# First out phase in 128x128 products with bursts of scores; nine loads of later quads moved behind the second out phase

## The chip, the cores and the metric

The kernel runs on one core of a Trainium2 chip. The metric is the device time of one execution in microseconds, the median of several runs. A core has five engines with queues of their own: PE (TensorE, matmuls), DVE (VectorE), ACT (ScalarE), POOL (GpSimd) and SP (SyncE). Here POOL issues the loads from HBM and SP the stores and the transposing DMAs.

## The reference

Sigmoid attention over 8 batches, 12 heads, 448 positions and 64 columns a head, followed by a feed-forward layer with a SiLU:

```
scores = q @ k.T / sqrt(64) - log(448)          per batch and head
x      = sigmoid(scores) @ v                    heads side by side: 3584 x 768
h      = x @ w_in                               768 x 2048
out    = (h * sigmoid(h)) @ w_out               2048 x 768, float32
```

The kernel holds its operands in float16 and sums in float32.

## The kernel before

**Attention.** The heads of a batch are taken four at a time, a quad: 24 quads, three to a batch. A quad's k and q come in by DMA (`kf`, `qf`, four buffers each), are copied into another order (`kr`, `qr`, L166, by DVE or ACT) and transposed by a DMA on SP's queue (`kT`, `qT`, L167). Scores come in tiles, seven to a quad (`scores`, L173): four matmuls of 64x64 with 448 columns fill one of two score buffers `psc` (L182), and ACT's sigmoid (L189) turns it into `attnT`, of which there are twelve. When a quad has its seven tiles, 28 matmuls of 64x64 (a set of value matmuls, L214) multiply them by v (`vf`, three buffers) into two banks `pav`, and DVE or ACT move these to `xT` (L226, L230).

**Feed-forward.** It goes by pairs of batches, m = 0 to 3. An h stage makes `gTr`, the SiLU of h; an out phase multiplies it by `w_out`. For m = 0 the h stage is plain (`h_unit`, L285, 128x128 matmuls `ph` of 448 columns, 189 ns a step); from m = 1 it is `h_pair` (L345), which forms the four blocks of a product by seven products of sums (`hx`, `hy`, `hz`, L361), as the out phase does as well: a set of seven products of 8 steps each (`out_set`, L491), with sums `S1` to `S4` of blocks of `gTr` made by DVE before them (`jobs`, L501) and the results gathered in `osb` by DVE (`plus`, L514; `end1` to `end7`). There are three sets in an out phase, and a fourth for m = 1 and 3. The fifth product of a set writes to `osb[1]`.

**Two forms of a product.** `alone` (L601) runs one product as 8 matmuls of 128x128 with 384 columns. `two` (L624) runs two products side by side as 64 matmuls of 64x64 (`side_by_side`, L248, L264), 16 steps of four. An attention tile, also 64x64, can be put between any two steps of a pair. In the kernel before only the first `FIRST_ALONE[m]` = 1 products of an out phase, and what is left over at its end, run alone (the last phase, without attention, wholly).

**The order** is written out by the program: `all_moe` is a generator that emits the feed-forward step by step with an estimate of its ns (163 a product step, 189 an h step), and the code around it emits attention tiles between the steps. Batches 0 and 1 come first, and attention of batches 2m and 2m + 1 is then laid into the h stage and the out phase of the pair before. Two ways of laying it in matter here:

- bursts (`bursts_to`, `attend`, `share`, L925 to L950): two tiles at once, or two tiles, the value set of a full quad and a third tile, then a stretch of dense steps, the stretches sized so that the bursts are evenly spread. They are used among 128x128 work.
- `deal` (L864): one tile at a time between the steps of pairs, by a due time and an estimate of when ACT is free (`sigmoid[-2]`), with a value set at the turn of a pair.

Before, the attention of batches 2 and 3 (46 tiles: quads 6 to 11 and four tiles of quad 12) starts with six tiles in bursts within the h stage and goes on by `deal` through the first out phase. The other phases use `deal`.

**Loads.** When q of quad g has been transposed, POOL makes a copy of one element (`seen`, L799), which waits for that transpose, and then issues k and q of quad g + 3. When the value set of quad g is emitted, `after_values` (L775) issues v of quad g + 3. In `h_pair` the first four rounds each emit one k or q copy of the coming quads (`late`, L376), k by ACT.

DVE's sums for the next set are emitted in `ended` (L587), as soon as the product that frees their buffer ends.

Of the kernel before, what the change touches and what calls it, by code (L numbers as in the profile page):

```python
# [19 lines left out]
def kernel(  # L20
# [140 lines left out]

    def dma_transpose(g, name, copy):
        if ("k", g) not in qkT:
            new_qkT(g)
        rows = p2.tile([P, NCH, 2, D], F16, tag=f"{name}r", name=f"{name}r")
        copy(rows, flat[name, g].rearrange("p j c d -> p c j d"))  # L166
        nc.sync.dma_start_transpose(  # L167
            out=qkT[name, g], in_=rows.rearrange("p c j d -> p (c j d)")
        )
# [294 lines left out]
    def w_sums():  # L464
# [3 lines left out]
        for f0 in range(0, NHC, NHC // 2):  # L468
            for o, x, y in (
# [5 lines left out]
                for f in range(f0, f0 + NHC // 2, 2):  # L475
                    nc.vector.tensor_sub(o[:, f : f + 2], x[:, f : f + 2], y[:, f : f + 2])
                    yield

    kept = cpool.tile([P, NFC, P], F16, tag="kept", name="kept")

# [10 lines left out]
    def out_set(a1, rows1, a2, rows2, scale, tail=(), last=False, halves=False, early5=False):  # L491
# [90 lines left out]
        return products, jobs  # L582

    free = {1: 0, 2: 0, 3: 0, 4: 0}
    jobs_to_do = []

    def ended(products):  # L587
        nonlocal vector_at
        for product in products:
            if product[5]:  # L590
                free[product[5]] += 1
        while jobs_to_do and free[jobs_to_do[0][0]] > 0:
            tag, job = jobs_to_do.pop(0)
            free[tag] -= 1
            job()
            vector_at = max(vector_at, clock) + 700
        while chores:
# [26 lines left out]
    def two(products, extras):  # L624
# [20 lines left out]
        yield 163  # L645

    rows_at = {14: (6, "k"), 16: (6, "q"), 18: (7, "k"), 21: (7, "q")}
    early = [h_unit(0, fc) for fc in range(2)]
# [27 lines left out]
    def out_products(m, tail):  # L676
        scale = ISX if m == 0 else 1.0
        for g in (0, 2, 4):
            of_set, jobs = out_set(
# [10 lines left out]
            for i, product in enumerate(of_set):  # L690
                extra = None
                if m % 2 == 0 and g == 2 and i < 4:
                    extra = partial(keep_part, scale, i)
                elif m == 0 and g == 2:
                    extra = partial(next, in_sums)
                elif m == 0 and g == 0 and i < 3:
                    extra = partial(list, islice(sums, 2 if i == 0 else 1))
                yield product, extra
        if m % 2 == 1:
# [9 lines left out]
            jobs_to_do.extend(jobs)  # L709
            for product in of_set:  # L710
                yield product, None

    def all_moe():
        for m in range(B // 2):
            tail = []
# [18 lines left out]
    def stretch(ns):  # L734
        nonlocal done, due
        due += ns
        while done < due or hold:
            step_ns = next(stream, None)
            if step_ns is None:
                break  # L740
            done += step_ns

    first_q = load_first_q()
# [31 lines left out]
    def after_values(g):  # L775
# [8 lines left out]
        elif g == 2:  # L784
# [11 lines left out]
    def rows_of_quad(g, name, copy):  # L796
        dma_transpose(g, name, copy)
        if name == "q" and g + 3 < NQB:
            nc.gpsimd.tensor_copy(seen, qkT["q", g][:1, NCH - 1, P - 1 :])  # L799
# [6 lines left out]
    def rows_if_any():  # L806
        if later:
            rows_of_quad(*later.pop(0), nc.vector.tensor_copy)

# [54 lines left out]
    def deal(n, stop, end, lead):  # L864
# [18 lines left out]

        for at in range(n, stop):
            due = start + (end - start) * (at - n + AHEAD) / (stop - n)
            while True:
                turn()
                if place == "turn" and room():
                    break
                if room() and done >= due and (clock >= sigmoid[-2] or done >= due + SLIP) and not hold:  # L890
                    break
                if place == "end":
                    rows_if_any()
                    place = None
                advance()
            between = place == "turn"
            if at % 2:
                rows_if_any()
# [9 lines left out]
            if ch == NCH - 3 and g % 6 < 4 and g + 3 < NQB:  # L908
                later.extend(((g + 3, "k"), (g + 3, "q")))
            if between and waiting and clock >= max(waiting[0][1], banks_at):  # L910
# [6 lines left out]
    def advance():  # L917
        nonlocal done, clock
        ns = next(stream)
        done += ns  # L920
        clock += ns

    AHEAD, SIGMOID, SLIP, DEBUG = 0.5, 850, 1e9, 0
    SWITCH, TILE, ROUND, SPARE = 200, 190, 190, 2400
# [39 lines left out]

    FIRST_ALONE = {0:1,1:1,2:1,3:1}
    WAIT = {1: 0, 2: 1300, 3: 1300}
    EXTRA = {1: 4, 2: 4, 3: 0}
    IN_H, LEAD, BEFORE = 6, {1:0,2:2600,3:2600}, {1:3200,2:2600,3:3000}
    sets = 7 * NHC * 163
    h_at = (2 * NFC * NCC - 8) * 189 + 3 * sets  # L970
    n = 2 * NT_B
    for m in range(1, B // 2):
        stop = min(2 * (m + 1) * NT_B + EXTRA[m], len(units))
        if m == 1:
            bursts = bursts_to(n, n + IN_H)
            for at, (burst, full) in enumerate(bursts):
                attend(burst, full)
                if at:
                    rows_if_any()
                if at == 1:  # L980
                    rows_if_any()
                for g, ch in burst:
                    n += 1
# [12 lines left out]
        seen_pairs = pairs_of  # L996
        while m < B // 2 - 1 and pairs_of == seen_pairs:
            advance()
# [33 lines left out]
```

## Time and profile before

| | us |
|---|---|
| runs | 361.05, 360.62, 360.23; median 360.62 |
| profiled execution | 362.33 |
| its span, first to last instruction | 360.6 |
| granted TensorE clock | 1.00 throughout |
| first h stage, with bursts (from 23.3) and dense | 23.3 to 74.5 |
| first out phase (m = 0) | 74.5 to 123.0 |
| second h stage (`h_pair`) | 123.0 to 156.2 |
| second out phase (m = 1) | 156.2 to 212.0 |
| third h stage | 212.0 to 245 |
| third out phase (m = 2) | 245 to 288 |
| fourth h stage and last out phase, no attention left | 288 to 360.6 |

The stages are read from the starts of PE's matmuls. Busy time of PE is the modelled time of its matmuls, which overlap, so rates are better read from start to start; "PEld" are weight loads. "issue" as a releaser means that the engine waited for nothing the profile shows. The DMA share is the mean busy share of the 16 DMA engines and can exceed 1, since packets overlap. Queue 0 carries POOL's loads, queue 1 SP's stores and transposes, queue 8 PE's instructions.

### The profile page before, as it was taken

What the parts mean: (1) busy time and instruction counts of PE and PEld (TensorE: products, weight loads), DVE (VectorE), ACT (ScalarE), POOL (GpSimd) and SP (SyncE); (2) the same over time, 40 slices, a digit from 0 to 9 for tenths busy, and PEclk for the clock granted to TensorE, in tenths of its full rate; (3) what the DMA queues carried; (4) which work ended last, traced back from release to release, by engine and by line L of the source; (5) the groups of instructions that cost most, each with busy time, mean ns of one, the idle gap of its engine ahead of it and who ended that gap; (6) DMA issues with size and microseconds to landing.
All of it is one profiled execution on the core that took longest, in us unless ns stands there. A gap on an engine that the chain in (4) does not pass through costs nothing.

```text
span 360.6 us, 10787 instructions
## 1 busy us (share of the span) xinstructions
PE 348.8 (97%) x4605; PEld 214.2 (59%) x4605; DVE 259.9 (72%) x487; ACT 247.5 (69%) x363; POOL 62.4 (17%) x105
## 2 busy tenths in 40 slices
PE   8999999999989999999997999999999999999995
PEld 4544445467777555567775765556787745555653
DVE  2547689897695578787755758787866677787663
ACT  5998977778776677687885667759889766660000
POOL 8545300604223001102203200210110000000000
PEclk9999999999999999999999999999999999999999
DMA  8999999999999446306899952731795030003333
GB/s 136 198 206 205 210 207 196 167 182 128 207 159 234 86 97 105 53 2 114 159 133 212 193 116 51 104 51 31 83 188 115 4 87 2 0 0 90 87 89 87
DMA packets 63919, 43.00 MB, mean 119 GB/s; under 512 B 36096, under 2 KB 60928, under 8 KB 63872
## 3 DMA queue, kind: packets, MB, share of 16 engines
q0 software_dynamic: 24896, 22.58, 42.3%
q1 hardware_dynamic: 38592, 19.21, 28.8%
q8 instruction: 36, 0.59, 0.7%
q10 hardware_dynamic: 384, 0.52, 0.4%
q14 instruction: 11, 0.09, 0.1%
HBM read 45.61 MB, written 11.01 MB: 157 GB/s over the span
## 4 chain that ended last, share of the span: by engine, by line
PE 88%; ACT 7%; issue 2%; DMA 1%; DVE 1%; ACTq 0%; POOLq 0%
PE po L264 21%; PE po L609 12%; PE hy L361 11%; PE ph L285 11%; PE psc L182 9%; PE pav L214 8%; PE hx L361 8%; PE hz L361 8%; ACT attnT L189 6%; DMA kf<-in_k_dram 1%; PE ptrq L151 1%; DVE osb L514 1%; PE ptrk L151 1%; DVE qT L158 0%; ACT m L529 0%
## 5 line engine op out<-in xcount | busy, mean ns | idle before, releaser
L189 ACT ACTIVATE attnT<-psc 128x896 f16<-128x896 f32 x168 | 143.5, 928 | 27.3 <-PE psc L182 26.1
L264 PEld LDWEIGHTS <-S 64*64 64x64 f16 x1248 | 58.2, 107 | 13.6 <-issue 2.8
L182 PE MATMUL psc<-qT,kT 64*64 64x448 f16 x672 | 64.1, 355 | 1.3 <-DVE qT L158 0.4
L264 PE MATMUL po<-T,S 64*64 64x384 f16 x640 | 53.2, 323 | 0.2 <-issue 0.2
L264 PEld LDWEIGHTS <-gTr 64*64 64x64 f16 x800 | 43.1, 107 | 9.6 <-issue 2.3
L514 DVE SCALAR_TENSOR_TENSOR osb<-po,osb 128x384 f32<-128x384 f32 x70 | 37.6, 554 | 15.0 <-PE po L264 9.7
L264 PE MATMUL po<-w_out_sb,S 64*64 64x384 f16 x608 | 44.6, 323 | 1.3 <-issue 1.2
L361 PEld LDWEIGHTS <-w_in_sb 128*128 128x128 f16 x288 | 28.0, 98 | 26.5 <-issue 0.6
L372 ACT ACTIVATE gTr<-u 128x448 f16<-128x448 f32 x48 | 27.6, 575 | 23.1 <-DVE u L385 19.1
L230 DVE TENSOR_SCALAR xT<-pav 128x448 f16<-128x448 f32 x44 | 25.6, 619 | 23.5 <-PE pav L214 23.5
L264 PE MATMUL po<-w_out_sb,gTr 64*64 64x384 f16 x480 | 40.5, 324 | 1.0 <-issue 1.0
L214 PE MATMUL pav<-attnT,vf 64*64 64x448 f16 x672 | 39.4, 350 | 2.0 <-issue 1.9
L285 PE MATMUL ph<-xT,w_in_sb 128*128 128x448 f16 x192 | 39.0, 353 | 0.0
L182 PEld LDWEIGHTS <-kT 64*64 64x64 f16 x672 | 26.5, 105 | 17.9 <-issue 10.9
L361 PE MATMUL hy<-xs,w_in_sb 128*128 128x448 f16 x144 | 35.1, 352 | 0.0
L264 PE MATMUL po<-T,gTr 64*64 64x384 f16 x320 | 34.3, 323 | 0.7 <-issue 0.7
L361 PE MATMUL hx<-xT,w_in_sb 128*128 128x448 f16 x144 | 34.6, 353 | 0.0
L361 PEld LDWEIGHTS <-W 128*128 128x128 f16 x216 | 21.1, 98 | 19.9 <-DVE osb L514 0.5
L214 PEld LDWEIGHTS <-vf 64*64 64x64 f16 x672 | 23.4, 106 | 10.9 <-issue 4.5
L514 DVE SCALAR_TENSOR_TENSOR osb<-po,m 128x384 f32<-128x384 f32 x32 | 17.2, 554 | 16.8 <-ACT m L529 6.4
L285 PEld LDWEIGHTS <-w_in_sb 128*128 128x128 f16 x192 | 17.6, 98 | 18.8 <-issue 3.6
L91 POOL DMA_DIRECT2D vf<-in_v_dram x24 | 17.1, 716 | 52.2 <-PE psc L182 42.6
(84 smaller groups left out, 481.0 us busy)
## 6 DMA issues: line engine op xcount, KB each, us to landing
out_dram<-osb SPq DMA_DIRECT2D x46, 192.0 KB, 4.0
vf<-in_v_dram POOLq DMA_DIRECT2D x24, 224.0 KB, 7.4
kf<-in_k_dram POOLq DMA_DIRECT2D x23, 224.0 KB, 6.1
qf<-in_q_dram POOLq DMA_DIRECT2D x23, 224.0 KB, 7.0
w_in_sb<-in_moe_w_in_dram POOLq DMA_DIRECT2D x8, 384.0 KB, 11.4
w_out_sb<-in_moe_w_out_dram POOLq DMA_DIRECT2D x4, 768.0 KB, 17.0
out_dram<-osb SPq DMA_DIRECT2D x17, 96.0 KB, 2.2
kT<-kr SPq DMA_TRANSPOSE x18, 5.8
```

Source lines behind the costliest of these rows:

```text
L91: nc.gpsimd.dma_start(flat[name, g][:, :, c0:c1].rearrange("p j c d -> p j (c d)"), rows_in(name, g)[:, :, c0 * D : c1 * D],)
L151: nc.tensor.matmul(ptr[j * D : (j + 1) * D, (c - c0) * P : (c - c0 + 1) * P], flat[name, g][:, j, c, :], ident, start=True, stop=True,)
L182: nc.tensor.matmul(psc[own, j, :S], qkT["k", g][rows, ch, own], qkT["q", g][rows, :, own], start=True, stop=True,)
L189: nc.scalar.activation(attnT[g, ch], psc[:, :, :S], AF.Sigmoid, bias=NEG_LOG_S, scale=QKSCALE)
L214: nc.tensor.matmul(pav[half][j * D : (j + 1) * D, :S], flat["v", g][own, j, ch, :], at[own, j, :], start=(ch == 0), stop=(ch == NCH - 1),)
L230: nc.vector.tensor_scalar_mul(xT[b][:, half * NQ + iq, :], pav[half][:, :S], SX)
L264: mm = nc.tensor.matmul(ps[lane ^ turn][own], a[rows, own], b[rows], start=(turn == c == 0), stop=(turn == 1 and c == count - 1), skip_gro ...
L285: nc.tensor.matmul(ph[:, :S], w_in_of[:, cc // NQ, cc % NQ, fc * P : (fc + 1) * P], xT[b][:, cc, :], start=(at == 0), stop=(at == NCC - 1),)
L361: nc.tensor.matmul(ps, a[:, c, i * P : (i + 1) * P], bs(c), start=(first and c == 0), stop=(c == HCC - 1), skip_group_check=True,)
L372: nc.scalar.activation(gTr[:, side * NHC + i, odd * S : (odd + 1) * S], src, AF.Silu, scale=ISX)
L514: nc.vector.scalar_tensor_tensor(out=o, in0=po, scalar=sign * scale, in1=x, op0=ALU.mult, op1=ALU.add)
L609: nc.tensor.matmul(po, a[:, fc, :], w[:, fc, :], start=(fc == 0), stop=(fc == NHC - 1))
```

## The change

In the first out phase all 21 products run alone, in 128x128 matmuls, and all 46 tiles of batches 2 and 3 are laid in as bursts (20 of them: four in the h stage, sixteen in the out phase). The loads of k and q of quads 19, 20, 21 and of v of quads 18, 19, 20 no longer follow the transposes and value sets of the second out phase: POOL issues them one after the other during the last product of its last set, behind a copy of one element of `osb[1]` (`mark`), which waits for that set's fifth product. v of quads 16 and 17 are issued after the value sets of quads 14 and 15 instead of 13 and 14. DVE's sums are emitted at the fourth step of a product, at most two at a time, and in the first and last out phase also when a product ends; extras move from the third to the fourth step. `deal` asks for at least one step between two tiles, and in the second out phase starts 400 ns earlier. Names that have no effect as set (`HALVES`, `GRID`, `EASE`, the parts of a transpose) are left out below.

```diff
+            first_done.append(osb[1])                     # in end5
...
+    AT_STEP, PER_TURN, prompt = 3, 2, False
     def ended(products):
         for product in products:
             if product[5]:
                 free[product[5]] += 1
-        while jobs_to_do and free[jobs_to_do[0][0]] > 0:
+        if prompt:
+            sums_if_any(4)
+
+    def sums_if_any(most):
+        while most and jobs_to_do and free[jobs_to_do[0][0]] > 0:
             tag, job = jobs_to_do.pop(0)
...
-            if fc == 2 and extra:
-                extra()
+            if fc == AT_STEP:
+                if not between:
+                    sums_if_any(2)
+                if extra:
+                    extra()
...
-            if at in (2, NHC + 2) and extras[at // NHC]:
-                extras[at // NHC]()
+            if at in (AT_STEP, NHC + AT_STEP):
+                sums_if_any(PER_TURN)
+                if extras[at // NHC]:
+                    extras[at // NHC]()
...
+                yield product, partial(load_behind, m) if m in BEHIND and i == BEHIND_AT else None
...
+            prompt = m in PROMPT
...
-        elif 4 < g < NQB - 3:
+        elif 4 < g < NQB - 3 and g not in VALUES_OF:
             load("v", g + 3)
+        for of in VALUES_OF.get(g, ()):
+            load("v", of)
...
+    BEHIND = {1: (("kq", 19), ("kq", 20), ("kq", 21), ("v", 18), ("v", 19), ("v", 20))}
+    VALUES_OF = {13: (), 14: (16,), 15: (17,), 16: (), 17: ()}
+    def load_behind(m):
+        nc.gpsimd.tensor_copy(mark, first_done[-1][:1, :1])
+        for names, g in BEHIND[m]:
+            load(names, g)
...
-        if name == "q" and g + 3 < NQB:
+        if name == "q" and g + 3 < NQB and g + 3 not in BEHIND_KQ:
             nc.gpsimd.tensor_copy(seen, qkT["q", g][:1, NCH - 1, P - 1 :])
...
-                if room() and done >= due and (clock >= sigmoid[-2] or done >= due + SLIP) and not hold:
+                if room() and done >= due and moved and (clock >= sigmoid[-2]) and not hold:
...
-    FIRST_ALONE = {0:1,1:1,2:1,3:1}
-    WAIT = {1: 0, 2: 1300, 3: 1300}
+    FIRST_ALONE = {0: 21, 1: 1, 2: 1, 3: 1}
+    PROMPT, WAIT, BURSTS = (0,3), {1: 0, 2: 900, 3: 1300}, (1,)
...
-        if m == 1:
-            bursts = bursts_to(n, n + IN_H)
+        if m in BURSTS:
+            bursts = bursts_to(n, stop)
             for at, (burst, full) in enumerate(bursts):
                 attend(burst, full)
...
-                    stretch(share(bursts[at:], 2 * NFC * NCC * 189 - 8 * 189 - 1134 - 400 - done))
-            while 1 not in h_done or place != "turn" and done < 0:
-                advance()
-        deal(n, stop, h_at - BEFORE[m], LEAD[m])
+                    stretch(share(bursts[at:], h_at - SPARE - done))
+        else:
+            deal(n, stop, h_at - BEFORE[m], LEAD[m])
```

More of the change, by code (lines that the diff above doesn't have):

```diff
@@ L596, in ended @@
             vector_at = max(vector_at, clock) + 700
+            most -= 1
         while chores:
@@ L734, in stretch @@
     def stretch(ns):
-        nonlocal done, due
+        nonlocal done, due, clock
         due += ns
@@ L807, in rows_if_any @@
         if later:
-            rows_of_quad(*later.pop(0), nc.vector.tensor_copy)
+            g, name, *part = later.pop(0)
+            rows_of_quad(g, name, nc.vector.tensor_copy, *part)
     keep_busy(0, 4)
@@ L889, in deal @@
                     break
-                if room() and done >= due and (clock >= sigmoid[-2] or done >= due + SLIP) and not hold:
+                if room() and done >= due and moved and not GRID < since < 16 and (clock + EASE >= sigmoid[-2]) and not hold:
                     break
@@ L908, in deal @@
             if ch == NCH - 3 and g % 6 < 4 and g + 3 < NQB:
-                later.extend(((g + 3, "k"), (g + 3, "q")))
+                later.extend(
+                (g + 3, name, *part)
+                for name in "kq"
+                for part in (((0, 4), (4, NCH)) if m in HALVES else ((),))
+            )
             if between and waiting and clock >= max(waiting[0][1], banks_at):
@@ L917, in advance @@
     def advance():
[L918 removed]
+        nonlocal done, clock, since
         ns = next(stream)
         done += ns
+        since = 0 if place == "turn" else since + 1
         clock += ns
[L923 removed]
+    AHEAD, SIGMOID, GRID, EASE, DEBUG = 0.5, 850, 99, 0, 0
+    since = 0
     SWITCH, TILE, ROUND, SPARE = 200, 190, 190, 2400
@@ L996 @@
         seen_pairs = pairs_of
-        while m < B // 2 - 1 and pairs_of == seen_pairs:
+        if m + 1 in BURSTS:
+            due = done
+            stretch(3000)
+        while m < B // 2 - 1 and m + 1 not in BURSTS and pairs_of == seen_pairs:
             advance()
```

43 lines of the change are left out of this document (29 added, 14 removed).

## The prediction

> **What bounds it now.** I read the page first: who is busy, what the last chain is made of, and the DMA queues.
>
> ```profile
> PE 348.8 (97%) x4605; PEld 214.2 (59%) x4605; DVE 259.9 (72%) x487; ACT 247.5 (69%) x363; POOL 62.4 (17%) x105
> ...
> q8 instruction: 36, 0.59, 0.7%
> ...
> PE 88%; ACT 7%; issue 2%; DMA 1%; DVE 1%; ACTq 0%; POOLq 0%
> ```
>
> TensorE (PE) carries the kernel, so the time is its work plus the stretches in which it starts nothing. The small "issue" share is time in which PE waits for nothing the profile names. Next the windows, one per out phase that has attention work in it:
>
> ```profile
> core 0: us, PE busy (x) PEld busy (x) DVE busy (x) ACT busy (x) POOL busy (x), PEclk, DMA share, GB/s
> 74.50:123.00 48.50, 45.54 (x978) 34.32 (x977) 36.22 (x74) 37.43 (x47) 12.15 (x21) 1.00 1.15 168
> 156.20:212.20 56.00, 53.54 (x1178) 39.37 (x1178) 38.82 (x76) 41.28 (x52) 10.58 (x18) 1.00 0.83 135
> 245.00:288.00 43.00, 42.66 (x962) 32.59 (x960) 30.97 (x63) 36.89 (x48) 2.11 (x3) 1.00 0.57 88
> ```
>
> PE idles about 3 us in the first and 2.5 us in the second, 0.3 us in the third; the DMA share (1.15, 0.83, 0.57) falls in the same order. The chain, asked for stretches of the first and second, says where:
>
> ```profile
> 103.65 0.46 PE po L264 x9
> 104.11 0.98 issue
> 105.08 0.51 PE po L264 x6
> ...
> 111.17 0.76 issue
> ...
> 117.81 0.68 issue
> ```
>
> ```profile
> 189.05 1.12 issue
> 190.17 1.30 PE pav L214 x21
> ...
> 196.06 1.22 issue
> ```
>
> These stops have one cause, read from two lists. Counted along PE's own list of instructions (9,241, weight loads included), the six longest stops of the out phases fall at positions 2498, 2755, 3010, 3267 and 5315, 5570: always 256 (within 2) or a multiple apart. Queue 8 moves 36 packets of 16,384 bytes, and 36 x 256 = 9,216, so one packet is 256 instructions. The packets of these stops landed at 96.88, 103.56, 110.36, 117.20, 188.88 and 195.76 us, and PE went on 1.3 to 1.6 us after each. So PE had run out of instructions. A packet started about when PE passed the place 256 earlier where there was little other traffic (within 0.7 us of it at 161.34, 178.23 and 246.51), but 4.0 to 4.6 us after it in these six cases, where loads, stores and transposes filled the queues. Wait, transfer (0.9 to 1.1) and restart add to 6.3 to 7.1 us; 256 instructions of the out phase last 5.4 to 6.2 us when nothing stops them. Against the dense spacing (162.5 ns a step of products, 189 a score tile, 1,324 a set of 28 value matmuls) the stops cost 0.51 + 1.20 + 0.99 + 0.87 = 3.57 us in the first phase and 1.34 + 1.41 = 2.75 in the second.
>
> **The change, part by part.**
>
> Products. Twenty products of the first out phase go from pairs of 64x64 matmuls to 128x128. A pair takes 16 steps of 162.5 ns, 2.60 us; two products alone 16 of 162.6 (the 1.30 us of one in the trace). No direct gain. PE's list loses 960 of its 9,241 instructions, all of them here.
>
> Bursts. A 64x64 score tile among 128x128 work costs a change of mode. The bursts of the stage before show it, by the starts:
>
> ```profile
> 31.69 1.88 PE L285 MATMUL ph<-xT,w_in_sb 128*128 128x448 f16 x9
> 33.50 0.57 PE L182 MATMUL psc<-qT,kT 64*64 64x448 f16 x8
> 34.00 0.58 PE L151 MATMUL ptrk<-ident,kf 128*64 128x128 f16 x14
> ```
>
> Nine h steps last 1.81 us instead of 9 x 0.189 = 1.70; eight score matmuls (two tiles) 0.50 instead of 0.38: 0.105 + 0.125 = 0.23 us a burst. From 66.44, where both orders are still the same, to the first hx matmul the new order holds 33 h steps (6.24), 46 tiles (8.69), 6 value sets (7.94), 168 product steps (27.32), together 50.19 us, and 20 bursts at 0.23, 4.60: 54.79 us. Before took 56.53 (66.44 to 122.97): 50.19 of the same work, 3.57 for instructions, 0.78 for its three bursts and the entry, and 2.0 in small waits of 0.1 to 0.5 us, nearly all at a score tile whose buffer the sigmoid (928 ns, against 0.84 from tile to tile) had not freed. Part sum: 54.79 - 56.53 = **-1.74**. It needs two covers. Instructions: about 21 a us instead of 40, so 256 last 12 us against the 7.1 at worst. Sigmoids: two tiles and ten steps are 2.21 us of PE, and two sigmoids 1.86 of ACT; the products' copy (485 ns) tops this in three bursts only. If it fails, each burst pays (rivals). The DVE work is the same 36.2 us in some 46.
>
> Loads moved. At the second phase k and q of quads 19, 20, 21 (six loads) were issued at 178.5, 190.9 and 197.5, v18 to v20 at 198.9, 201.5 and 209.2; all nine now stand behind the last product set, and v16, v17 one value set later. Left in the phase are k, q of 18 and three v loads, beside stores and transposes. The third phase is the nearest row for that mix: three v loads, the same stores and transposes, the same density. There the packet waited at most 1.83 us and no stop came at a 256 mark. So I take the whole 2.75: **-2.75**. Its ends are 0 (stores and transposes alone hold the packet up) and -3.1 (with the 0.34 us wait for evictions at 199.16, right after the second stop).
>
> What the moved loads now wait for. POOL's new copy waits for the eviction of the last set's fifth product (DVE, done at about 211.45 in the old times, 0.6 before the h stage at 212.04). Queued behind it on POOL are the nine issues, 0.71 us each, then the copy and loads of quads 22 and 23, which ran at 225 and later, so POOL has room. The first reader is ACT's copy of k19, at 217.44. Issued at about 211.95, k has 5.5 us. The six k loads from 166 on landed in 3.7 to 6.5, median 4.4. ACT can slip about 1.1 us more: it idles 0.20 after that copy, and its last operation of the round ends at 220.15, the matmul that needs it (hz of the next round) starting at 221.1. I take 0; bounds 0 and 2.0 (8.5 us from issue to landing, the longest of a k load in the first out phase). q19 is read at 221.4, k20 at 225.5: more room each. v16 and v17 follow a value set (some 8 us) later and are read 8 to 16 us on, landing taking 7.4: 0, at worst 1.
>
> Order inside the later phases. DVE's sums go in at the fourth step of a product instead of at its end, a tile needs a step of products before it, the start of the deal moves by 0.4 us. The sums are still a whole pair (2.6 us) ahead of their reader, the engine work is unchanged: 0, within 0.4 either way.
>
> Sum: -1.74 - 2.75 = -4.5. The profiled execution took 362.33 us (span 360.56, 1.77 around it), so 357.8 for it; the median of the runs is 360.62, 1.7 lower, and the same difference gives **356.1**.
>
> **Rivals.**
>
> The second phase keeps its stops (16%): stores and transposes alone hold the packet up. For: from 186 to 194 their queue 1 took a share of 1.0 to 1.3 of the DMA engines, the loads' queue 0 almost none, and both stay. Against: they had piled up behind the loads of 178.5 to 186.7, and the third phase has the same stores and transposes, up to a share of 1.5, without a stop. Then only the first part counts: 360.62 - 1.74 = 358.9. The Trainium skill, "Runtime: NRT & Kernel Launch", "Instruction fetch mechanics", stands on this side: crossing a 16 KiB block of 256 instructions is said to be mostly hidden, as fetching outruns dispatch; by that rule moving loads frees nothing. The six stops disagree with it, the other 30 crossings show no stop over 0.3 us and agree.
>
> k19 comes late (7%): that longest landing, 8.5 us, puts ACT 3.0 behind, 1.9 beyond its slack, and hz waits: 358.0.
>
> The bursts give nothing (8%): sigmoids lag by 0.11 us a burst, 16 x 0.11 = 1.74: 357.9.
>
> Slower (9%): the bursts bind on the two score buffers. Sixteen bursts in the out phase ask for two buffers at once, where before one tile came at a time. From 0.28 us of waiting a burst the whole 4.5 is gone; at 0.52, the longest wait before a tile in the old phase, it is 8.3 lost: 364.4. Against: in 23.3 to 52.9 ACT was busy 26.03 of 29.60 us and the bursts there ran dense.
>
> **How the numbers follow.** The forecast has 60%, its own range 355.1 (evictions and small waits gone as well) to 357.4. With k19 and the idle bursts (to 358.0) that is 75%; the first rival, 358.9, is needed for 8 in 10, so the range is 355.0 to 359.1. A measurement here tells about 0.2%, 0.7 us, from no change: all cases but the last lie over that, less 2% for cases that meet: faster 0.89, same 0.02, slower 0.09.
>
> **What would show it.** Right: no stop over 0.5 us at 256 marks in either phase; the stretch to the first hx of 54.8 us instead of 56.5; the second out phase about 2.7 us shorter; ACT's copy of k19 not waiting for a DMA. Wrong: "issue" pieces of about a microsecond in the chain of the second phase, score matmuls waiting for ACT at each burst of the first, or a gap before hz some 9 us into the third h stage.

## The result and the profile after

The changed kernel takes 359.2 us (median of 21 runs, 358.08 to 361.34) beside 361.21 us for the kernel before in the same set (21 runs, 359.15 to 366.79). The ratio is 0.9945, 95% interval 0.9923 to 0.9967, so about 2.0 us were gained where 4.5 were forecast, and 359.2 lies just above the range (355.0 to 359.1). A second set of 12 runs gave 0.9948 (0.9915 to 0.9982). All ratios leave out executions more than 1.5% above the fastest of their kernel, and the profiles that are named below "after, old loads", "before, loads moved" (the first) and "loads moved, q8 ahead" are such slow executions. The profiled execution of the changed kernel took 361.34 us, with a span of 359.6.

The page of the changed kernel, the rows that answer to those shown of before (busy time of PE, the instruction queue, the last chain by engine):

```profile
PE 351.4 (98%) x4125; PEld 201.6 (56%) x4125; DVE 259.9 (72%) x487; ACT 248.3 (69%) x363; POOL 62.3 (17%) x103
...
q8 instruction: 32, 0.52, 0.6%
...
PE 88%; ACT 4%; DVE 4%; issue 1%; DMA 1%; ACTq 0%; POOLq 0%
```

PE has 480 matmuls less (and as many weight loads), which are four instruction packets less. "issue" fell from 2% to 1%, and DVE stands in the chain with 4% where it had 1%: something new waits for DVE. The windows, one per out phase (the columns are the engines' busy us and counts, the granted clock, the DMA share and GB/s):

```profile
core 0: us, PE busy (x) PEld busy (x) DVE busy (x) ACT busy (x) POOL busy (x), PEclk, DMA share, GB/s
76.56:123.33 46.77, 46.63 (x489) 23.38 (x488) 35.51 (x73) 37.19 (x46) 12.16 (x21) 1.00 1.03 166
156.56:209.97 53.41, 52.91 (x1177) 37.75 (x1177) 38.60 (x76) 40.76 (x52) 4.09 (x8) 1.00 0.64 103
242.97:287.03 44.06, 43.12 (x962) 32.28 (x961) 30.82 (x63) 37.15 (x48) 2.10 (x3) 1.00 0.55 86
```

By its busy time PE no longer idles in the first out phase (0.14 us) and hardly in the second (0.50), but it now does in the third: 0.94 us, where it was 0.3. For the third phase the forecast had no change.

For everything that follows the time is cut by fixed places in the work. T0 is the start of ACT's 17th sigmoid of the first h stage (55.77 us before), ahead of all that the change touches. Stage 1 goes from T0 to the first hx matmul of the second h stage, stage 2 from there to the first hx of the third (second h stage and out phase), stage 3 to the first hx of the fourth, stage 4 to the end. Of the two first profiles:

| us | start to T0 | stage 1 | stage 2 | stage 3 | stage 4 | T0 to end |
|---|---|---|---|---|---|---|
| before | 55.77 | 67.20 | 89.08 | 75.98 | 72.54 | 304.79 |
| after | 57.30 | 66.03 | 86.64 | 77.06 | 72.52 | 302.25 |
| difference | +1.53 | -1.17 | -2.43 | +1.08 | -0.02 | -2.54 |

The first column is the same work in both kernels; the first k load landed 4.12 us after its issue instead of 3.49, and the score tiles of the chain took 0.52 us each up to 10 us, instead of 0.34 to 0.41. The forecast had -1.74, -2.75 and 0 for the three stages. The changed kernel's chain in the third out phase shows one of the new losses (start, length, what; "issue" is again the time in which PE waits for nothing that is shown):

```profile
264.89 0.16 PE po L268 x4
265.06 0.94 PE pav L218 x20
266.00 0.41 issue
266.41 0.57 PE pav L218 x8
```

The stop is at list position 6595, which is 195 above a multiple of 256: an instruction packet that came late. It had waited 3.86 us from the moment it was due (when PE passed the place 256 earlier). In the first profile of before no packet of this phase waited over 1.83 us; in each of the other three, made later, one waited about 3 us, with a stop of 0.1 us at most. The other loss is at the end of the same phase:

```profile
280.58 1.14 DVE xT L234 x2
281.72 0.31 DVE xs L318
282.06 0.40 DVE xs L318
282.55 0.24 issue
282.79 0.38 DVE xs L318
283.17 0.48 DVE osb L519
283.68 0.57 DVE osb L519
284.29 1.49 PE pav L218 x26
```

The last value set needs a PSUM bank that the two `osb` evictions free. In the new order DVE first does the `xs` differences for the next pair (`chores`), and the set starts 0.44 us late; the products behind it lose 0.15 us more than before (0.28 against 0.13).

### The profile page after: what moved, and what is told of

Same layout as the page of the kernel before. It is cut to its first block, busy times and chain, and to the rows that moved or that the text cites. A ratio compares the mean times of both kernels' runs of the same rounds, so it can differ in the third digit from the quotient of the medians.

```text
span 359.6 us, 9826 instructions
## 1 busy us (share of the span) xinstructions
PE 351.4 (98%) x4125; PEld 201.6 (56%) x4125; DVE 259.9 (72%) x487; ACT 248.3 (69%) x363; POOL 62.3 (17%) x103
## 4 chain that ended last, share of the span: by engine, by line
PE 88%; ACT 4%; DVE 4%; issue 1%; DMA 1%; ACTq 0%; POOLq 0%
PE po L621 19%; PE po L268 13%; PE hy L365 11%; PE ph L289 11%; PE psc L186 9%; PE pav L218 8%; PE hz L365 8%; PE hx L365 8%; ACT attnT L193 4%; DVE osb L519 2%; DMA kf<-in_k_dram 1%; PE ptrk L151 1%; DVE xs L318 1%; DVE xT L234 1%; PE ptrq L151 1%
## 5 line engine op out<-in xcount | busy, mean ns | idle before, releaser
L186 PE MATMUL psc<-qT,kT 64*64 64x448 f16 x672 | 60.2, 360 | 1.0 <-DVE qT L158 0.4
L268 PEld LDWEIGHTS <-S 64*64 64x64 f16 x864 | 38.3, 107 | 9.8 <-PE po L268 1.1
L268 PE MATMUL po<-T,S 64*64 64x384 f16 x448 | 36.4, 323 | 0.0
L186 PEld LDWEIGHTS <-kT 64*64 64x64 f16 x672 | 21.6, 105 | 20.9 <-issue 14.7
L621 PEld LDWEIGHTS <-S 128*128 128x128 f16 x232 | 22.0, 98 | 17.6 <-issue 3.9
L268 PEld LDWEIGHTS <-gTr 64*64 64x64 f16 x544 | 28.1, 107 | 6.2 <-PE po L268 0.9
L268 PE MATMUL po<-w_out_sb,S 64*64 64x384 f16 x416 | 30.4, 323 | 0.0
L218 PEld LDWEIGHTS <-vf 64*64 64x64 f16 x672 | 22.1, 106 | 11.5 <-issue 3.3
L268 PE MATMUL po<-w_out_sb,gTr 64*64 64x384 f16 x320 | 27.0, 324 | 0.0
```

The costliest lines, as they stand in the source:

```text
L186: nc.tensor.matmul(psc[own, j, :S], qkT["k", g][rows, ch, own], qkT["q", g][rows, :, own], start=True, stop=True,)
L218: nc.tensor.matmul(pav[half][j * D : (j + 1) * D, :S], flat["v", g][own, j, ch, :], at[own, j, :], start=(ch == 0), stop=(ch == NCH - 1),)
L268: mm = nc.tensor.matmul(ps[lane ^ turn][own], a[rows, own], b[rows], start=(turn == c == 0), stop=(turn == 1 and c == count - 1), skip_gro ...
```

## The experiments

Each run below has one profile, and most were also timed against the kernel before on the same chip; three kernels were profiled more than once. Theory A, the one I started from: stops come where a 256 mark of the list meets data traffic, and the new list has put marks of the later phases on other places of the work. B: the new order of DVE's sums and of the tiles makes the differences. C and D concern the spread: executions of one kernel differ by several us, C because a load is waited for, D because the packets vary. All profiles, with the stages as above:

| kernel | T0 | stage 1 | stage 2 | stage 3 | T0 to end | ratio to before (interval) |
|---|---|---|---|---|---|---|
| before, four profiles | 55.77 | 67.20 | 89.08 | 75.98 | 304.79 | 1 |
| | 55.63 | 68.03 | 88.07 | 75.98 | 304.66 | |
| | 57.41 | 68.44 | 88.26 | 76.04 | 305.31 | |
| | 55.73 | 68.07 | 87.81 | 75.99 | 304.43 | |
| after, three profiles | 57.30 | 66.03 | 86.64 | 77.06 | 302.25 | 0.9945 (0.9923 to 0.9967) |
| | 55.72 | 66.14 | 85.88 | 76.54 | 301.08 | 0.9948 (0.9915 to 0.9982) |
| | 55.74 | 68.55 | 85.89 | 77.29 | 304.27 | |
| after, old loads | 55.63 | 66.03 | 91.17 | 77.30 | 307.04 | 0.9987 (0.9952 to 1.0022) |
| before, loads moved | 56.12 | 69.68 | 86.42 | 75.99 | 304.64 | 0.9915 (0.9874 to 0.9956) |
| the same again | 55.43 | 70.94 | 86.42 | 75.98 | 305.93 | 0.9953 (0.9921 to 0.9985) |
| before, new order | 55.54 | 68.16 | 87.84 | 76.44 | 304.97 | 0.9999 (0.9959 to 1.0040) |
| after, old order | 55.62 | 66.96 | 86.70 | 75.99 | 302.20 | 0.9964 (0.9932 to 0.9997) |
| after, marks moved | 56.36 | 66.41 | 85.89 | 76.45 | 301.28 | 1.0007 (0.9938 to 1.0075) |
| before, marks moved | 55.43 | 68.39 | 86.86 | 75.98 | 303.81 | 1.0063 (1.0030 to 1.0096) |
| after, q8 ahead | 55.73 | 68.08 | 85.90 | 77.35 | 303.87 | 1.0010 (0.9950 to 1.0069) |
| loads moved, q8 ahead | 55.40 | 71.17 | 86.42 | 75.98 | 306.16 | 0.9996 (0.9911 to 1.0081) |
| after, differences behind | 56.44 | 67.20 | 86.67 | 75.92 | 302.36 | 0.9970 (0.9943 to 0.9997) |
| both repairs | 55.95 | 66.75 | 86.81 | 75.85 | 301.96 | 0.9944 (0.9914 to 0.9974) |
| old order, marks moved | 55.85 | 67.16 | 87.19 | 75.98 | 302.91 | 0.9947 (0.9911 to 0.9983) |
| differences behind in stage 3 only | 55.99 | 66.05 | 85.89 | 76.21 | 300.70 | 0.9933 (0.9903 to 0.9964) |

**The changed kernel with the old loads.**

```diff
-    BEHIND, VALUES_OF = {1: (("kq", 19), ("kq", 20), ...)}, {13: (), 14: (16,), 15: (17,), ...}
+    BEHIND, VALUES_OF = {}, {}
```

> The changed kernel with the six k/q loads and the v loads back where the kernel before has them; every list of TensorE, VectorE and ScalarE stays that of the changed kernel. Theory A (marks: each phase is slowed by the instruction packets that wait behind data traffic at its 256 marks, so a phase is fast only if its loads are away from its marks): stage 1, from T0 to the first hx of the second pair, stays at 66.0 us; stage 2 gets its stops back and is 88.5 to 89.5 us instead of 86.64; stage 3 keeps its 1.08 us; time about 2.4 us above the changed kernel, within 0.3% of the kernel before. Rival B (order: the gain of stage 2 comes from the new order of sums and evictions, not from the loads): stage 2 stays at 86.6 us and the time within 0.2% of the changed kernel.

Stage 1 is 66.03 again, and stage 2 has its stop back, in one piece. Its chain in the second out phase:

```profile
191.13 0.65 PE po L268 x15
191.78 3.67 issue
195.45 0.35 PE po L268
```

Packet 16 waited 6.90 us; three loads (184.0 to 185.4 us) and two transposes (184.5 and 185.9) had been issued just ahead of it. With the loads back the second phase is slow again although the order is the new one: A. The size was missed (91.17 instead of 88.5 to 89.5), and that shows how far one such stop can go. The ratio, 0.9987, agrees with A.

**The kernel before with only the loads moved**, PE's, DVE's, ACT's and SP's lists as before. The edit is against the changed kernel, whose `BEHIND` and `VALUES_OF` stay.

```diff
-    FIRST_ALONE = {0: 21, 1: 1, 2: 1, 3: 1}
+    FIRST_ALONE = {0: 1, 1: 1, 2: 1, 3: 1}
-    AT_STEP, PER_TURN, prompt = 3, 2, False
+    AT_STEP, PER_TURN, prompt = 2, 0, False
...
-    PROMPT, WAIT, BURSTS, HALVES = (0,3), {1: 0, 2: 900, 3: 1300}, (1,), ()
+    PROMPT, WAIT, BURSTS, HALVES = (0,3), {1: 0, 2: 1300, 3: 1300}, (), ()
```

> The kernel before with its own order on TensorE, VectorE, ScalarE and SyncE, only the six k/q loads and the v loads moved behind the last set of the second out phase. Theory A (marks): stage 2 falls from 89.08 by 2.4 to 2.8 us, stage 1 stays at 67.2 and stage 3 at 76.0 because the marks lie where they lay, so the whole gain is 2.4 to 2.8 us, a ratio of 0.9925 to 0.9935. Rival B (order): less than 0.7 us of stage 2 goes, ratio 0.998 or more. Rival C (the moved loads themselves disturb the third phase): stage 2 falls as in A and stage 3 rises by 1 us, ratio about 0.996.

Stage 2 is 86.42 us, with no "issue" piece over 0.1 us in the chain of its out phase, and stage 3 is 75.99: no stop moves there (its rival C falls). So the loads are worth 1.9 us against the mean of the four profiles of before (88.30). The 0.9915 was confirmed only in part by a second set, made at the end:

> The kernel before with only the loads moved, as run already, for a second set of times and a second profile. If the loads carry the gain: stage 2 86.4 us, stage 3 76.0, stage 1 67 to 68.5 us as in the kernel before; ratio 0.993 to 0.995. If the moved products and bursts of the first phase matter as the profiles say, by 1.3 us, it lies 0.2 to 0.5 us above the changed kernel's ratio of 0.9945 once the third phase's 1.0 us is set against it; if the first set of times was right, 0.9915.

It gave 86.42 and 75.98 once more and 0.9953. The two sets together bracket the whole change's 0.9945, so in the times the moved loads alone can't be told from the whole change. The stage 1 of both these profiles (69.68 and 70.94) is longer than was expected, for a reason that both kernels share: PE waits 2.2 and 2.7 us for quad 8 (below), and its clock falls after that. So from T0 to the end neither profile is clearly shorter than the mean of before (304.64 and 305.93 beside 304.80); the gain of the moved loads shows in stage 2 and in the times.

**The kernel before with only the new order** (the names are those of the changed kernel).

```diff
-    AT_STEP, PER_TURN, prompt = 2, 0, False
+    AT_STEP, PER_TURN, prompt = 3, 2, False
-                if room() and done >= due and not GRID < since < 16 and ...
+                if room() and done >= due and moved and not GRID < since < 16 and ...
-    PROMPT, WAIT, BURSTS, HALVES = (0,3), {1: 0, 2: 1300, 3: 1300}, (), ()
+    PROMPT, WAIT, BURSTS, HALVES = (0,3), {1: 0, 2: 900, 3: 1300}, (), ()
```

> The kernel before with its own first out phase and its own loads, and only the new order: the sums taken one or two at a time at the third step of a product, the tiles of the later phases placed by the new rule. The TensorE list is as long as in the kernel before, so its marks lie where they lay. Theory A (marks): stage 3 is 76.0 us plus at most 0.45 for evictions that come behind the sums, stages 1 and 2 within 0.4 us of the kernel before, ratio 0.999 to 1.002. Rival B (order is what costs stage 3 its 1.08 us): stage 3 is 77.0 us and the ratio 1.003.

Stage 3 is 76.44: up by 0.46, PE waits 0.43 us ahead of its last value set for the evictions, and no packet stops it. A's number.

**The changed kernel with the old order** (the same edit backwards).

> The changed kernel with the old order of the sums, of the extra steps and of the later tiles; bursts, 128x128 products and moved loads stay, and so does the length of the TensorE list up to the first out phase. Theory A (marks): the stop in the third phase stays (0.4 to 0.8 us at a 256 mark), only the 0.44 us of the wait for evictions goes; stage 3 is 76.5 to 76.8 us, ratio to the kernel before 0.993 to 0.995. Rival B (order): stage 3 falls to 76.0 us, no stop over 0.2 us at a mark, and stage 1 loses its extra 0.5 us too: ratio 0.990.

Stage 3 is 75.99, without the wait and without the stop: here A was wrong by its own text, since the marks lie where the changed kernel has them. The packet of mark 24 waited 1.75 us and not 3.86. The ratio, 0.9964, lies above what either theory had. The two runs and the two kernels make a square: order old or new, marks old or new, stage 3 is 75.98, 76.44, 75.99 and 77.06 (the loads are moved where the marks are new; the run with the old loads, 77.30, and the one with only the loads moved, 75.99, show that this is not what matters here). The differences of x cost 0.46 with the new order; the stop came only with the new order and the new marks together, as far as single profiles can tell. What the traffic has to do with it can be guessed at from SP's list. In the changed kernel packet 24 was due at 260.1 us, when PE passed the place 256 earlier, and started at 263.9; SP's transposes around it:

```profile
259.00 1.33 SPq L171 DMA_TRANSPOSE qT<-qr  x1
261.82 1.22 SPq L171 DMA_TRANSPOSE kT<-kr  x1
263.15 2.48 SPq L171 DMA_TRANSPOSE qT<-qr  x1
```

With the old order it was due at 259.6 and started at 261.4:

```profile
258.43 1.39 SPq L171 DMA_TRANSPOSE qT<-qr  x1
261.25 2.69 SPq L171 DMA_TRANSPOSE kT<-kr  x1
264.04 1.24 SPq L171 DMA_TRANSPOSE qT<-qr  x1
```

The last k and q transposes are issued 1.33 us apart in the one and 2.79 in the other, and only in the one did the packet have to wait past both. All seven profiles with the new tiles and these marks show the pair back to back and a wait of 2.8 to 4.1 us for the packet; PE stopped over 0.3 us in five of them. That the pair is the cause was not tried.

**The changed kernel with its marks moved.** 192 more instructions ahead of the first out phase, in the first h stage (products of batch 1):

```diff
+            parts = 2 if b == 1 and NCC * fc + at < 96 else 1
+            for part in range(parts):
+                cols = slice(part * S // parts, (part + 1) * S // parts)
                 nc.tensor.matmul(ph[:, cols], ..., xT[b][:, cc, cols], ...)
```

As made here the cut spoils the first step of the cut sums, so part of h is not the reference's; the work and its length are those meant. In the later kernels with cut products the first step of each sum stays whole.

> The changed kernel with 96 of the products of the second h stage's first tile group cut in two halves of 224 columns, which puts 192 more instructions ahead of the first out phase and so moves every later 256 mark by 192 places earlier in the work; the order is that of the changed kernel. Theory A (marks and order together make the stop of the third phase: the new order issues the transposes of a k and a q back to back at the moment when a packet is asked for): the stop of 0.6 to 1.0 us at the 24th packet goes, stage 3 is 76.4 to 76.6 us, the 0.45 us for the evictions stay; time 0.3 to 0.7 us below the changed kernel apart from at most 0.6 us for the cut products. Rival B (the order alone makes it): stage 3 stays at 77.0 to 77.3 us with a stop at another mark.

Stage 3 is 76.45, no stop, the 0.44 us for the evictions still there: A's number. The times of that set are too few to say more.

**The kernel before with its marks moved**, by 128 instructions, in the same way.

> The kernel before with 64 products of the second h stage cut in two halves, which puts 128 instructions more on TensorE's list ahead of the first out phase and moves every later 256 mark half way to the one before. If the stops belong to the marks (an instruction packet that comes late), all stops over 0.3 us in the two out phases stand at the moved marks, half way between the old places of the work, and none at the old places; their sum stays between 2 and 6.5 us and the time within 0.5% of the kernel before. If they belong to the work at those places (a wait for data or for an eviction), they stay where they were in the work.

Its stops, by the position in PE's list of the matmul that came late, beside those of the four profiles of before:

```
before  1   2498 2755 3010 3267 | 5315 5570
before  2        2755      3267 | 5315 5570
before  3   2498 2755           | 5315 5570 6082
before  4   2498 2755 3010      | 5315 5570
moved       2243 2755      3523 | 5827
```

All are 194 or 195 above a multiple of 256, in the moved list too, where these positions are other work (2755 was a product matmul and is now one of a value set). So the stops belong to the list, not to the work. The time was missed: 1.0063 instead of within 0.5%. By the interval a shift of the marks that adds next to no work costs this kernel 1.1 to 3.5 us, but no trace shows where: the one profile is the fastest execution of its set (361.06 of 361.06 to 368.48 us), and its 303.81 from T0 to the end are less than the 304.80 of before.

**Second, third and fourth profile of the kernel before, second and third of the changed one**, nothing edited.

> The kernel before, unchanged, for a second profile. Theory A (the stops at the 256 marks recur with about the same size): stage 1, from T0 to the first hx of the second pair, 66.8 to 67.6 us with three or four stops of 1 us at its marks, stage 2 88.7 to 89.5 us with two stops of about 1.5 us. Rival D (the stops vary from execution to execution, and the profile that the forecast was made from had many): stage 1 between 65.5 and 66.8 us apart from a wait for the load of q8, with two stops or fewer, stage 2 87.5 to 88.7 us.

> The kernel before, unchanged, for a third profile. Reading 1 (the stops vary and the first profile had many): the instruction stops of the first and second out phase add up to 2.5 to 5 us here against 6.3 us in the first profile and 4.0 us in the second, and the wait for quad 8's rows is between 0 and 2.5 us. Reading 2 (the stops are the same each time): 6.0 to 6.6 us.

> The kernel before, unchanged, for a fourth profile; the expectations are those of the third: 2.5 to 5 us of instruction stops by reading 1, 6.0 to 6.6 us by reading 2.

> The changed kernel, unchanged, for a second profile and a second set of times. Theory A (order and marks together make the third phase's stop; the stops of the first phase are gone for good): stage 3 is 77.0 to 77.4 us with the stop at the 24th packet again, stage 1 65.9 to 66.5 us plus at most 1 us of wait for quad 8's rows, no stop at a mark in it, stage 2 85.9 to 86.7 us; ratio to the kernel before 0.992 to 0.997. Rival D (all stops are chance): stage 3 without the stop, 76.4 us, or a stop elsewhere.

> The changed kernel, unchanged, for a third profile. Reading 1: from T0 to the end 301 to 302.5 us, no instruction stop in the first out phase, 0 to 0.7 us of them in the second and 0 to 0.9 us in the third, no wait for quad 8's rows over 1 us. Reading 2: 302.2 us as in its first profile, with the same two stops of 0.6 us.

The places recur and the sizes don't; the second profile of before is as D had it. Against the dense spacing the stops at marks add up to 6.3, 4.0, 5.3 and 5.7 us in the four profiles of before, so reading 1 holds in part: they vary, but the last two lie above the 2.5 to 5 us that it had given. In stage 2 alone they are 2.75, 1.80, 1.96 and 1.53: the profile of the forecast had the most. The changed kernel has none in the first out phase in any of its three; in the second one of 0.6 us in one of three; in the third 0.63, 0.1 and 0.87 (so stage 3 of its second profile, 76.54, is nearly what D had). The third profile of after ends at 304.27, over what reading 1 had given, for this reason (its chain at the end of the first h stage):

```profile
67.26 7.97 DMA qf<-in_q_dram
75.23 0.02 issue
75.25 0.62 DVE qr L170
75.87 0.46 DVE w_out_sb L480
76.33 0.60 DVE S L345
76.94 0.55 DVE gTr L302
77.48 0.04 issue
77.52 1.46 PE po L621 x8
```

DVE's copy of quad 8's q rows stands ahead of the last `gTr` and waits for a load that is one of eight issued in a row (65.9 to 70.9 us); that costs PE 2.5 us. In the four profiles of before this costs 0, 2.2, 0 and 0.3 us, in the three of after 0, 0 and 2.5. Neither kernel's edit touches it.

**Quad 8's k and q ahead of quad 6's v**, in the changed kernel, and in the kernel before with the loads moved.

```diff
             if g == 6:
-                load("v", 6)
                 load("kq", 8)
+                load("v", 6)
                 load("v", 7)
```

> The changed kernel with the loads of quad 8's k and q issued ahead of quad 6's v instead of behind it. Theory C (part of the spread of both kernels is a wait of VectorE's copy of quad 8's q rows for its load at 70 to 75 us, which holds the gTr behind it and so TensorE, 0 to 2.5 us long and longer by the clock that falls while TensorE stands): the copy does not wait for the load, TensorE has no stop over 0.3 us from 70 to 77 us, the slowest of the runs lie below 360.5 us and the median is 0.3 to 1.2 us below the changed kernel's, ratio 0.991 to 0.994. Rival D (the spread comes from the instruction packets alone): median and spread as in the changed kernel, ratio 0.9945.

> The kernel before with only the loads moved behind the last set of the second out phase, and quad 8's k and q ahead of quad 6's v. Theory C: 0.5 to 1.5 us below the run with the loads moved alone, median 357.4 to 358.4 us, ratio 0.987 to 0.991, fastest of all kernels so far. Rival D: ratio 0.9915, as with the loads moved alone.

The copy follows its predecessor at once in both, so C names a real wait, but no gain is seen. In the first PE then stands 1.9 us at 98 us for the transpose of a later q; in the second the stops at two marks (98.8 and 108.1 us) are 1.41 and 3.81 us, and PE's clock falls during the second. A reading that was not tested: the traffic of the first out phase is late as a whole, and an engine that comes earlier meets it elsewhere. The ratios are inconclusive, with intervals of 0.6 and 0.9% to each side.

**The differences of x behind the evictions**, everywhere; with the marks moved as well; and the old order with the marks moved.

```diff
     def ended(products):
...
+        flush()            # the chores, taken out of sums_if_any
```

> The changed kernel with one line more in the order: the differences of x for the next pair are put on VectorE's list at the end of a product, behind the evictions, instead of between them. TensorE's list and the loads stay. If the wait of 0.44 us ahead of the value set and the 0.28 us behind it at the end of the third out phase come from those differences standing ahead of the evictions, both go and stage 3 is 0.5 to 0.7 us shorter, 76.4 to 76.8 us, with the stop at the 24th packet still there; ratio to the changed kernel 0.9983. If VectorE is late there for another reason, stage 3 stays at 77.1 to 77.3 us.

> The changed kernel with both repairs of the new order: 96 products of the second h stage cut in halves, which moves the later 256 marks by 192 places, and the differences of x behind the evictions. Theory A: stage 3 is 75.9 to 76.1 us, stage 2 85.9 to 86.3 us, stage 1 66.2 to 66.6 us; 1.2 to 1.8 us below the changed kernel, ratio to the kernel before 0.988 to 0.992. Rival D: stops come back at other marks, the time is that of the changed kernel within 0.5 us.

> The changed kernel with the old order of the sums, the extra steps and the later tiles, and the marks moved by 192 places. Theory A: stage 3 is 76.0 us, as with the old order in either place of the marks, stage 2 85.9 to 86.7 us, stage 1 66.2 to 66.9 us; ratio to the kernel before 0.988 to 0.993, within 0.3% of the kernel with both repairs. Rival D: as above, within 0.5 us of the changed kernel.

Stage 3 falls to 75.92, 75.85 and 75.98: the account of the third phase is closed. But stage 2 is 86.67 and 86.81 in the first two, where the changed kernel has 85.9 without a stop: twice in one value set, PE waits for evictions, 0.49 and 0.34 us (197.3 and 197.8 us in the first). The changed kernel waits there once, 0.24 us, and the kernel before with the loads moved twice, 0.31 and 0.34. So the new order had taken something away in the second phase that it gave back in the third. None of the three kernels beats the changed one in the times: the ratios, 0.9970, 0.9944 and 0.9947, miss what was expected (0.988 to 0.993) and are, in the last two, what D had. The profile of the second shows no stop at another mark, that of the third one of some 0.7 us in stage 2.

**Behind the evictions in the third out phase only.**

```diff
+        if at_end:         # at_end is m == 2
+            flush()
```

> The changed kernel with the differences of x put behind the evictions in the third out phase alone, not in the second. If the account of the stages holds: stage 1 66.0 to 66.3 us apart from a wait for quad 8's rows, stage 2 85.9 to 86.7 us, stage 3 75.9 us without a stop at the 24th packet or 76.6 with it; 0.5 to 1.2 us below the changed kernel, ratio to the kernel before 0.990 to 0.9935. If the account fails, stage 2 or stage 3 is where the changed kernel has it, and the ratio 0.9945.

Its chain at the end of the third out phase has no DVE in it:

```profile
281.58 1.32 PE pav L218 x28
282.91 1.30 PE po L268 x32
```

Stage 3 is 76.21 (mark 24 still costs 0.37), stage 2 85.89, and 300.70 us from T0 is the shortest of all profiles, as the account says. That is one profile, and the three of the changed kernel are up to 3.2 us apart. The ratio 0.9933 is the lowest of the kernels that hold the whole change; that it beats the changed kernel is not shown, the intervals overlap.

## Why the prediction was right and where it was wrong

**What bounds it** was right. The stops are late instruction packets, they sit at fixed positions of the list, and moving the list moves them. They go where PE uses fewer instructions a us (first phase) or where the loads go (second phase). In the changed kernel's first out phase a packet still waited about 3.7 us (from 110.6 to 114.2), but the 256 instructions ahead of it last 12.3 us there, and it landed more than 7 us before it was needed. The rule of the Trainium skill that stood on the rival's side ("Runtime: NRT & Kernel Launch", "Instruction fetch mechanics": crossing a 16 KiB block is mostly hidden) does not hold here where traffic is dense: one crossing cost 3.67 us of "issue" in the chain (old loads), and moving loads alone freed 1.9.

**Bursts, -1.74: the mechanism right, the term mis-sized.** A burst costs what was said: nine h steps and eight score matmuls of the changed kernel's first h stage last 1.81 and 0.50 us in its trace as well. No stop at a mark is left in the phase. The stretch to the first hx lasts 55.36 us (67.97 to 123.33) and not 54.79. The missing term is evictions, which the prediction had dismissed with DVE's work being the same in less time. The chain of the changed kernel in the first out phase:

```profile
107.85 1.00 DVE osb L519 x2
108.85 0.06 DVE S L509
108.91 0.46 issue
109.37 0.69 DVE w_in_sb L336
110.05 0.48 DVE osb L519
110.53 0.04 issue
110.57 1.51 PE pav L218 x26
```

A sum for the next stage (`w_in_sb`) stands between the evictions, and the value set waits 0.34 us; the scores behind it lose 0.18 and a later value set 0.12, 0.64 together. Over the profiles of the two kernels stage 1 is 67.94 in the mean before and 66.91 after, -1.0; without the wait for quad 8's rows 67.3 and 66.05, -1.3.

**Loads, -2.75: right in kind, too large.** Stage 2 went from a mean of 88.30 to 86.14, -2.2; moved alone, in the old order, -1.9. The 2.75 was one profile's sum, and the three profiles made since had 1.5 to 2.0. The reasoning on k19 held: it landed 4.44 us after its issue, and ACT's copy (L141, columns: start, length, engine, line, tiles, and in brackets a wait) has no wait:

```profile
214.90 0.58 ACT L376 ACTIVATE gTr<-u 128x448 f16<-128x448 f32 x1 [0.16 <-DVE u L437]
215.38 0.93 ACT L141 ACTIVATE kr<-kf 128x896 f16<-128x896 f16 x1
```

**Order inside the later phases, 0 within 0.4: the step that failed.** The prediction put the whole term at 0, since the sums stay a pair ahead of their reader and the engines' work is the same. Stage 3 grew from 76.0 to 77.06, 76.54 and 77.29, +1.0 in the mean. Two things were left out. The sums' function also flushes `chores`, so the differences of x came ahead of evictions (0.46). And the prediction counted marks only where stops were to vanish: a list shorter by 960 instructions, 3.75 packets, puts every later mark in other work, and with the new order a packet came late at one of them (0.5 in the mean of the three); that a k and a q transpose issued back to back hold it up was seen each time and not tested. In the second out phase the same order shortened a wait for evictions from 0.65 us (loads moved, old order) to 0.24, so there it gained 0.4 to 0.5 us that the forecast had not counted either.

**The sum.** Means of the profiles, T0 to end: 304.80 before, 302.53 after, -2.3 (stages -1.0, -2.2, +1.0, 0.0), in line with the -2.0 of the times. Of the 4.5 forecast 0.7, 0.6 and 1.0 are missing. These means are of four and three profiles, single ones of which differ by 0.9 and 3.2 us, so that they meet the times so closely is partly luck. The prediction also took the profile's difference off the median, although the profiled execution stood 1.7 us over that median and nothing said that this excess was not made of the very stops that were to go.

**The rivals.** The first, at 358.9, comes nearest in time but is not what happened: the second phase lost its stops. k19 was not late, the bursts were not idle, and they did not bind on the score buffers.

## What to carry to other kernels

Where PE runs short matmuls beside dense DMA traffic, count the instructions: each 256 want a packet, and any edit that changes their number moves all later packets into other work, so a phase that is not edited can gain or lose a microsecond. Before subtracting a stall, look at it in more than one profile; stalls that come from queues keep their places and change their sizes. A helper that is moved takes everything along that it flushes.

## What the runs showed of the hardware

The granted clock can fall after a long stop of PE, which makes the stop dearer than its length. The kernel with the loads moved, second profile, where PE waits for quad 8's rows from 74.3 to 77.0 us:

```profile
core 0: us, PE busy (x) PEld busy (x) DVE busy (x) ACT busy (x) POOL busy (x), PEclk, DMA share, GB/s
76.00:77.00 1.00, 0.00 (x0) 0.00 (x0) 1.00 (x3) 0.00 (x0) 0.00 (x0) 1.00 1.24 191
77.00:78.00 1.00, 0.99 (x7) 0.60 (x7) 1.00 (x2) 0.54 (x1) 0.00 (x0) 0.99 1.24 194
78.00:79.00 1.00, 1.00 (x7) 0.29 (x9) 1.00 (x3) 0.16 (x1) 0.00 (x0) 0.50 1.33 176
...
80.00:81.00 1.00, 1.00 (x20) 0.54 (x12) 1.00 (x3) 1.00 (x2) 0.00 (x0) 0.50 1.41 53
...
82.00:83.00 1.00, 1.00 (x28) 0.59 (x24) 0.00 (x0) 0.90 (x1) 0.18 (x1) 1.00 0.55 106
```

About 1 us after PE went on the clock was 0.50 for 3.4 us, and by that share the products and scores of that time took 1.7 us more. It happened in five profiles, in and after stops of 2.2, 2.4, 2.7, 3.5 and 3.7 us (from the end of one matmul to the start of the next); the clock fell 2.2 to 5.0 us after the stop had begun and was back 3.4 us later in four of them and 6.8 in one. It did not happen after stops of 1.9, 2.0 and 2.4 us in three others, so the length of the stop alone doesn't decide it.

Also not expected was how long one instruction packet of 16 KB can wait: 6.9 us in the second phase with the old loads, and 6.8 in the first phase of one kernel (before with the loads moved and q8 ahead).
